# VectorE's order in 73 steps of a talking-heads attention kernel: the maximum ahead of the emptying

## The chip, the cores and the metric

The program runs on one core of a Trainium2 chip. The metric is device time in microseconds (us) from start to end of one execution.

## What is computed

Attention with mixing over the heads, and behind it two matrix products with a squared ReLU in between. Batch 4, 12 heads, 448 positions, head size 64; 1792 tokens of 768 channels, hidden size 2048.

```python
scores = scale * np.matmul(q, k.transpose(0, 1, 3, 2))
scores = np.einsum('bhij,hg->bgij', scores, w_pre)
scores = scores - np.max(scores, axis=-1, keepdims=True)
attn = np.exp(scores)
attn = attn / (np.sum(attn, axis=-1, keepdims=True) + 1e-09)
attn = np.einsum('bhij,hg->bgij', attn, w_post)
x = np.matmul(attn, v)          # then (batch, seq, heads * head size)
...
h = x @ w_in
r = np.maximum(h, 0.0)
out = (s * (r * r) + b) @ w_out
```

## The kernel before

The rows of the queries are cut into 16 chunks of 110 or 118 rows (four to a batch), and each chunk into 11 or 12 blocks of up to 10 rows; there are 180 blocks. A block holds 10 rows times 12 heads, 120 partitions, by 448 keys. The mixing over heads is then one matrix product of a block with a 120 x 120 matrix.

Values that need more than one matmul pass of precision are kept as two parts, a rounded high part and the rest, the low part. ScalarE copies a tile out of PSUM and makes the high part, and VectorE makes the low part by a subtraction (`low_parts`, L236 to L239). So a transposed q (`Tq`) or k (`Tk`) is ready for its matmuls only when VectorE has done its low part.

The attention runs as one loop over steps `s`. A block goes through several steps:

- step t: `premix(t)`: three matmuls into `pm` (L602), the maximum of each row on VectorE (L604, `st<-pm`), the exponential on ScalarE (L609, `pm<-pm,st`), which also sums, and the scaled sum (L613, `st<-pm`).
- step t+1: `normalize(t)`: the reciprocal on VectorE (L621) and the scaled high part on ScalarE (L623, `eh`); then `remainder(t)`, the low part of `eh`, on VectorE (L630).
- step t+3: `postmix(t)`: twelve matmuls into one of two buffers `po` (L645).
- step t+4: `evacuate(t)`: the emptying of `po` into `A` on VectorE (L661; on ScalarE for the last chunk).

Between these stand pieces of other work by a plan that is made ahead: `qk_pair`, the scores of the next but one chunk for two heads (six matmuls, L503 `sc<-Tk,Tq`, copied by ScalarE, L513 `S<-sc`); `av_pair` (L531, `xp<-A,v`) in front of it in the same step; and, mostly in the steps between, `prep_q` or `prep_k`, the transposes (L478 `trq`, L458 `trk`) into the same single PSUM buffer `sc` that the scores use, with their high part by ScalarE (L482, L462) and their low part by VectorE (L239), which is put on a list `later` and issued at the next `low_parts()`. The planned `qk_pair` steps come in most places every second step:

```python
w0, w1 = first[ci - 1] - LD, first[ci] - LD
return [w0 + i for i in (1, 3, 5, 7, 9, w1 - w0 - 1)]
```

Each engine works its instructions in the order in which the code issues them. VectorE also converts weights for the later products in between (`conversion`, L158 to L181, at most one piece in a step, ahead of the reciprocal; 49 pieces before the tail, spread over about 139 steps). The relayout of the scores into blocks (`blk<-S`) is a DMA on SP's queue, and GpSimd splits each block into its two parts (`hl`, L587 and L588).

Of the kernel before, what the change touches and what calls it, by code (L numbers as in the profile page):

```python
# [21 lines left out]
def talking_heads_attention__then__act_relu2_kernel(  # L22
# [53 lines left out]
    NB = len(blocks)  # L76
# [109 lines left out]
    def place_w(n):  # L186
        w_pool[n].tile([P, 2, 3 * P], F32R, tag=f"w{n}", name=f"place_{n}", bufs=1)

    def convert_step(upto):

        if done["run"] is None:
            if done["conv"] >= min(upto, len(units)):
                return False
            done["run"] = conversion(done["conv"])
        try:
            next(done["run"])
        except StopIteration:
            done["run"] = None
            done["conv"] += 1
        return True  # L200
# [13 lines left out]
    def load_x(r, b, kc):  # L214
        raw = rp.tile([P, S], F32, tag="xraw", name=f"xraw_{r}_{b}_{kc}", bufs=NKC)
        nc.sync.dma_start(raw, xd[b][kc])
        xraw_t[r, b, kc] = raw

    def split_x(r, b, kc):
        raw = xraw_t.pop((r, b, kc))  # L220
        if b == 1:

            if kc % 2 == 0:
                x_u["g"] = mp.tile(
                    [P, 2, PT], F32R, tag=f"g{kc // 2}_1", name=f"xg_{r}_{kc}", bufs=1
                )
            x = x_u["g"][:, :, kc % 2 * S:kc % 2 * S + S]
        else:
            x = rp.tile([P, 2, S], F32R, tag="x", name=f"x_{r}_{b}_{kc}", bufs=NKC)
        nc.scalar.activation(x[:, 0, :], raw, AF.Copy)  # L230
        later.append((x[:, 1, :], raw, x[:, 0, :]))
        x_u[r, b, kc] = x
# [3 lines left out]
    def low_parts():  # L236
        while later:
            o, x, hi = later.pop(0)
            nc.vector.tensor_tensor(out=o, in0=x, in1=hi.bitcast(F32), op=ALU.subtract)  # L239
# [322 lines left out]
    def qk_pair(ci, p):  # L562
        low_parts()
        for m in range(3):
            qk_part(ci, p, m)
# [9 lines left out]
    def relayout(t):  # L575
        ci, i0, ni = blocks[t]
        blk = blkp.tile([BP, S], F32, tag="blk", name=f"blk_{t}", bufs=LD)
        nb = first[ci + 1] - first[ci]
        r = t - first[ci]
        nc.sync.dma_start(blk[:ni * H, :], s_t[ci][r:r + nb * (ni - 1) + 1:nb, :, :])  # L580
        blk_t[t] = blk

    def split(t):
        n = blocks[t][2] * H
        blk = blk_t.pop(t)
        hl = blkp.tile([BP, 2, S], F32R, tag="hl", name=f"hl_{t}", bufs=2)
        nc.gpsimd.tensor_scalar(hl[:n, 0, :], blk[:n], 1.0, 0.0, op0=ALU.mult, op1=ALU.add)  # L587
        nc.gpsimd.tensor_tensor(  # L588
            out=hl[:n, 1, :], in0=blk[:n], in1=hl[:n, 0, :].bitcast(F32), op=ALU.subtract
        )  # L590
        hl_t[t] = hl

    def premix(t):
        n = blocks[t][2] * H
        hl = hl_t.pop(t)

        tag = "px" if t % 3 == 2 else "pm"
        pm = ps.tile([P, 512], F32, tag=tag, name=f"pm_{t}", bufs=banks.count(tag))
        for _ in range(2 if t < first[1] - 1 else 1 if t < first[1] + 3 else 0):
            nc.tensor.matmul(pm, keep[:, :P], keep, start=True, stop=True)  # L600
        for m, (w, x) in enumerate(((wpre_lo, 0), (wpre_hi, 1), (wpre_hi, 0))):
            nc.tensor.matmul(pm[:n, :S], w[:n, :n], hl[:n, x, :], start=(m == 0), stop=(m == 2))  # L602
        st = smp.tile([BP, 4], F32, tag="st", name=f"st_{t}")
        nc.vector.tensor_reduce(  # L604
            out=st[:n, 0:1], in_=pm[:n, :S], axis=AX.X, op=ALU.max, negate=True
        )

        e = pm[:, :S]
        nc.scalar.activation(e[:n], e[:n], AF.Exp, bias=st[:n, 0:1], accum_out=pm[:n, S:S + 1])  # L609
        e_t[t] = (e, st)  # L610

        total = pm[:, S:S + 1]
        nc.scalar.activation(  # L613
            st[:n, 2:3], total[:n], AF.Copy, scale=2.0 ** -15, bias=1e-9 * 2.0 ** -15
        )

    def normalize(t):

        n = blocks[t][2] * H
        e, st = e_t[t]  # L620
        nc.vector.reciprocal(st[:n, 3:4], st[:n, 2:3])  # L621
        eh = blkp.tile([BP, 2, S], F16, tag="eh", name=f"eh_{t}", bufs=3)
        nc.scalar.activation(eh[:n, 0, :], e[:n], AF.Copy, scale=st[:n, 3:4])  # L623
        eh_t[t] = eh

    def remainder(t):
        n = blocks[t][2] * H
        e, st = e_t.pop(t)
        eh = eh_t[t]
        nc.vector.scalar_tensor_tensor(  # L630
            out=eh[:n, 1, :], in0=e[:n], scalar=st[:n, 3:4], in1=eh[:n, 0, :],
            op0=ALU.mult, op1=ALU.subtract,
        )

    def postmix(t):
        ci, i0, ni = blocks[t]
        n = ni * H
        eh = eh_t.pop(t)
        if i0 == 0:
            a_t[ci] = ap_.tile([P, NC, H, CH], F32, tag="A", name=f"A_{ci}")  # L640
        po = ps.tile([P, 512], F32, tag="po", name=f"po_{t}", bufs=2)
        for c in range(NC):
            j0 = min(c * P, S - P)
            for m, (x, y) in enumerate(((1, 0), (0, 1), (0, 0))):
                nc.tensor.matmul(  # L645
                    po[:, c * BP:(c + 1) * BP],
                    eh[:n, x, j0:j0 + P],
                    wpost[:n, y].rearrange("p g i -> p (g i)"),
                    start=(m == 0),
                    stop=(m == 2),  # L650
                )
        po_t[t] = po

    def evacuate(t):
        ci, i0, ni = blocks[t]
        dst = a_t[ci][:, :, :, i0:i0 + ni]
        src = po_t.pop(t)[:, :NC * BP].rearrange("p (c g i) -> p c g i", c=NC, g=H)[:, :, :, :ni]
        if ci == NCH - 1:
            nc.scalar.activation(dst, src, AF.Copy)  # L659
        else:  # L660
            nc.vector.tensor_copy(dst, src)  # L661
# [6 lines left out]
    XA = 3  # L668
# [3 lines left out]
    plan, load = [], {}  # L672
# [95 lines left out]
    def run_plan(step, early):  # L768

        k0 = state["next"]  # L770
        while k0 < len(plan) and plan[k0][0] < step + 1:
            _, order, _, f, args = plan[k0]
            if (order == 0) == early:
                f(*args)
            k0 += 1
        if not early:
            state["next"] = k0
            copy_x()
# [55 lines left out]
    while plan[0][0] < 0:  # L834
        x = plan.pop(0)
        x[3](*x[4])
        low_parts()
    tail = first[NCH - 1]
    for s in range(NB + 4):
        if s == tail - LD:  # L840
            early.close()
            rp = ctx.enter_context(tc.tile_pool(name="rp", bufs=1, side="right", reuse_waits="tile"))
            rp.tile([P, S], F32, tag="xraw", name="place_xraw", bufs=NKC)
            for n in range(NU_EARLY, NU_EARLY + NU_TAIL):
                w_pool[n] = rp
                place_w(n)
            rp.tile([P, X_GAP // 4], F32, tag="gap", name="gap_x", bufs=1)
            rp.tile([P, 2, S], F32R, tag="x", name="place_x", bufs=NKC)
            rp.tile([P, END_GAP // 4], F32, tag="end", name="gap_end", bufs=1)
        if s + LD < NB:  # L850
            relayout(s + LD)
        if s + LS < NB:
            split(s + LS)
        if 0 <= s - 1 < NB:
            ops = 7 * NU_EARLY
            if not later and turn["ops"] < ops * (s - CONV0) / (tail - LD - 2 * NP - CONV0):
                turn["ops"] += convert_step(NU_EARLY)
            normalize(s - 1)
        if 0 <= s - 4 < NB:
            evacuate(s - 4)  # L860
        if s <= tail - XA:
            low_parts()
        if s < NB:
            premix(s)
        low_parts()
        if s < 2:
            (build_scale, build_post)[s](*loaded_consts)
            qk_pair(1, NP - 2 + s)
        if 0 <= s - 1 < NB:
            remainder(s - 1)  # L870
        run_plan(s, True)
        if 0 <= s - 3 < NB:
            postmix(s - 3)
        run_plan(s, False)
        if 0 <= s - (tail - LD) < NKC // 2:
            for kc in range(2):
                load_x(0, 0, 2 * (s - (tail - LD)) + kc)
        if 0 <= s - (tail - XA) < NKC:
            split_x(0, 0, s - (tail - XA))
        if 0 <= s - tail < NKC:  # L880
            load_x(0, 1, s - tail)
# [111 lines left out]
```

## Time and profile before

| | us |
|---|---|
| time, median of 3 runs (936.03 to 936.42) | 936.33 |
| time of the profiled execution | 936.44 |
| its span from first to last instruction | 934.7 |
| TensorE (PE) busy in it | 913.4 |
| VectorE (DVE) busy | 655.5 |
| ScalarE (ACT) busy | 567.1 |
| GpSimd (POOL) busy | 396.6 |

TensorE's granted clock is 1.00 in every part of the profile, the higher of its two levels. The attention loop fills about the first 470 us; then come the two matrix products, each in two halves. Busy time of TensorE is modelled at the ends of matmuls, so spacing from start to start says more than the printed gaps.

### The profile page before, as it was taken

To read this page: it belongs to the slowest core of one execution; us is meant where nothing else is said; L and a number is where in the kernel's file an instruction comes from. 1 tells how busy PE (TensorE), PEld (TensorE's weight loads), DVE (VectorE), ACT (ScalarE), POOL (GpSimd) and SP (SyncE) were. 2 spreads that over 40 slices of the span, in tenths; PEclk is the share of its full clock that TensorE was granted. 3 is DMA by queue.
4 is the path that set the end of the run, shared out by engine and by line. 5 is a ranking of instruction groups with operands and counts; after the bars stand their busy time and mean duration, and the time that the engine had idled before them with its cause. 6 is when DMAs were issued, how large, how long until landed. Compare 5 with 4: busy or idle time off the path is not lost.

```text
span 934.7 us, 19915 instructions
## 1 busy us (share of the span) xinstructions
PE 913.4 (98%) x7538; PEld 785.5 (84%) x7538; DVE 655.5 (70%) x1366; ACT 567.1 (61%) x1266; POOL 396.6 (42%) x452
## 2 busy tenths in 40 slices
PE   8899999999999999999999999999999999999998
PEld 5567777777777777777799999999999999999998
DVE  4888888889888898889688149966306924976211
ACT  5778788887888878888876877121117687700000
POOL 4776676666766666777523233000002333300000
PEclk9999999999999999999999999999999999999999
DMA  5755546564465635646324122353510420245321
GB/s 128 183 153 129 164 117 163 147 158 134 132 171 153 150 119 141 169 114 192 95 75 153 61 64 81 102 172 115 177 51 18 149 88 18 82 155 186 128 87 58
DMA packets 126556, 115.22 MB, mean 123 GB/s; under 512 B 63960, under 2 KB 122348, under 8 KB 126460
## 3 DMA queue, kind: packets, MB, share of 16 engines
q1 hardware_dynamic: 116934, 102.28, 39.5%
q10 hardware_dynamic: 9366, 11.59, 3.5%
q8 instruction: 59, 0.97, 0.5%
q0 software_dynamic: 160, 0.09, 0.1%
q14 instruction: 37, 0.30, 0.1%
HBM read 58.87 MB, written 16.52 MB: 81 GB/s over the span
## 4 chain that ended last, share of the span: by engine, by line
PE 62%; ACT 20%; DVE 11%; DMA 4%; issue 1%; POOL 0%; SPq 0%; ACTq 0%; DVEq 0%
PE po L311 25%; PE ph L254 24%; ACT pm L609 7%; ACT S L513 5%; ACT eh L623 4%; DVE A L661 4%; DMA blk<-S 4%; PE pm L602 4%; DVE st L604 3%; PE sc L503 3%; PE xp L531 3%; PE po L645 2%; ACT st L613 2%; ACT xs L553 1%; PE ph_head L254 1%; DVE Tq L239 1%
## 5 line engine op out<-in xcount | busy, mean ns | idle before, releaser
L311 PE MATMUL po<-w,g 128*128 128x384 f32 x1344 | 233.5, 336 | 0.0
L311 PEld LDWEIGHTS po<-w,g 128*128 128x128 f32 x1344 | 233.0, 188 | 0.3 <-ACT ob L318 0.3
L588 POOL TENSOR_TENSOR hl<-blk,hl 120x448 fp32r<-120x448 f32 x180 | 205.8, 1143 | 15.0
L272 POOL TENSOR_TENSOR g<-h,g 128x448 fp32r<-128x448 f32 x64 | 79.4, 1241 | 280.0 <-ACT g L271 260.2
L254 PE MATMUL ph<-x,w 128*128 128x448 f32 x810 | 164.1, 362 | 0.0
L254 PEld LDWEIGHTS ph<-x,w 128*128 128x128 f32 x810 | 151.9, 187 | 10.3
L587 POOL TENSOR_SCALAR hl<-blk 120x448 fp32r<-120x448 f32 x180 | 104.6, 581 | 120.5 <-PE pm L602 105.5
L645 PEld LDWEIGHTS <-eh 120*128 120x128 f16 (+1 forms) x2160 | 115.3, 98 | 40.8 <-issue 40.5
L645 PE MATMUL po<-wpost,eh 120*128 120x120 f16 (+1 forms) x2160 | 144.6, 217 | 1.4 <-ACT A L659 1.4
L609 ACT ACTIVATE pm<-pm,st 120x448 f32<-120x448 f32 x180 | 110.0, 611 | 56.6 <-DVE st L604 56.2
L630 DVE SCALAR_TENSOR_TENSOR eh<-pm,st,eh 120x448 f16<-120x448 f32 x180 | 122.3, 679 | 26.2 <-ACT eh L623 22.9
L623 ACT ACTIVATE eh<-pm,st 120x448 f16<-120x448 f32 x180 | 114.4, 636 | 15.4 <-DVE st L621 15.0
L604 DVE TENSOR_REDUCE st<-pm 120x1 f32<-120x448 f32 x180 | 110.6, 615 | 7.2 <-PE pm L602 6.9
L661 DVE COPY A<-po 128x480 f32<-128x480 f32 x168 | 107.0, 637 | 0.1
L602 PE MATMUL pm<-hl,wpre_hi 120*120 120x448 f32 x360 | 101.9, 364 | 0.7 <-POOL hl L588 0.7
L531 PE MATMUL xp<-A,v 128*64 128x110 f32 (+1 forms) x1536 | 93.5, 265 | 0.0
L503 PE MATMUL sc<-Tk,Tq 64*110 64x448 f32 (+1 forms) x576 | 82.7, 393 | 8.0 <-DVE Tq L239 5.0
L513 ACT ACTIVATE S<-sc 110x896 f32<-110x896 f32 (+1 forms) x91 | 83.1, 914 | 9.5 <-PE sc L503 6.5
L602 PE MATMUL pm<-hl,wpre_lo 120*120 120x448 f32 x180 | 82.8, 460 | 0.1
L531 PEld LDWEIGHTS xp<-A,v 128*64 128x64 f32 x1536 | 74.2, 136 | 9.6 <-issue 0.9
L318 ACT ACTIVATE ob<-po 128x384 f32<-128x384 f32 x28 | 13.8, 491 | 98.0 <-PE po L311 84.3
L602 PEld LDWEIGHTS pm<-hl,wpre_hi 120*120 120x120 f32 x360 | 65.4, 182 | 5.6 <-POOL hl L588 1.0
(81 smaller groups left out, 979.5 us busy)
## 6 DMA issues: line engine op xcount, KB each, us to landing
blk<-S SPq DMA_DIRECT2D x172, 210.0 KB
raw<-in_moe_w_in_dram SPq DMA_DIRECT2D x32, 384.0 KB
raw<-in_moe_w_out_dram SPq DMA_DIRECT2D x32, 384.0 KB
xraw<-xd SPq DMA_DIRECT2D x48, 224.0 KB
part<-ob ACTq DMA_DIRECT2D x28, 192.0 KB
acc<-part SPq DMA_DIRECT2D x28, 192.0 KB
out_dram<-acc ACTq DMA_DIRECT2D x28, 192.0 KB
v<-in_v_dram SPq DMA_DIRECT2D x24, 192.0 KB
```

The source lines that it names most:

```text
L254: nc.tensor.matmul(ph[:, :S], w[:, i, c0:c0 + P], x[:, y, :], start=(kc == 0 and m == 0), stop=(kc == NKC - 1 and m == 2),)
L311: nc.tensor.matmul(po[:, :NO], g[:, x, c0:c0 + P], w[:, y, :], start=(f == 0 and m == 0), stop=(f == NF - 1 and m == 2),)
L513: nc.scalar.activation(s_t[ci][:n, 2 * p:2 * p + 2, :], x_t["two"][:n, :, :S], AF.Copy, scale=SCALE)
L531: nc.tensor.matmul(xp[e * D:(e + 1) * D, p % 4, :n], vt[:, e, c, :], a[:, c, 2 * p + e, :n], start=(c == 0), stop=(c == NC - 1),)
L588: nc.gpsimd.tensor_tensor(out=hl[:n, 1, :], in0=blk[:n], in1=hl[:n, 0, :].bitcast(F32), op=ALU.subtract)
L602: nc.tensor.matmul(pm[:n, :S], w[:n, :n], hl[:n, x, :], start=(m == 0), stop=(m == 2))
L604: nc.vector.tensor_reduce(out=st[:n, 0:1], in_=pm[:n, :S], axis=AX.X, op=ALU.max, negate=True)
L609: nc.scalar.activation(e[:n], e[:n], AF.Exp, bias=st[:n, 0:1], accum_out=pm[:n, S:S + 1])
L623: nc.scalar.activation(eh[:n, 0, :], e[:n], AF.Copy, scale=st[:n, 3:4])
L630: nc.vector.scalar_tensor_tensor(out=eh[:n, 1, :], in0=e[:n], scalar=st[:n, 3:4], in1=eh[:n, 0, :], op0=ALU.mult, op1=ALU.subtract,)
L645: nc.tensor.matmul(po[:, c * BP:(c + 1) * BP], eh[:n, x, j0:j0 + P], wpost[:n, y].rearrange("p g i -> p (g i)"), start=(m == 0), stop=(m = ...
L661: nc.vector.tensor_copy(dst, src)
```

## The change

`pairs` are the steps in which the plan has a `qk_pair`; `full` are those of them that stand behind a step without one, up to the tail. In a full step VectorE gets its maximum (in `premix`) first, then the low parts, then the emptying of `po`. In all other steps the order stays emptying, low parts, maximum.

```diff
     tail = first[NCH - 1]
+    pairs = {x[0] for x in plan if x[3] is qk_pair}
+    full = {s for s in pairs if s - 1 not in pairs and s <= tail - XA}
     for s in range(NB + 4):
...
             normalize(s - 1)
-        if 0 <= s - 4 < NB:
-            evacuate(s - 4)
-        if s <= tail - XA:
-            low_parts()
+        if s not in full:
+            if 0 <= s - 4 < NB:
+                evacuate(s - 4)
+            if s <= tail - XA:
+                low_parts()
         if s < NB:
             premix(s)
         low_parts()
+        if s in full and 0 <= s - 4 < NB:
+            evacuate(s - 4)
```

There are 73 full steps; in 45 of them low parts stand between the maximum and the emptying. The instructions of PE, ACT, POOL and SP keep their order word for word, apart from the numbers in buffers' names; only VectorE's rows move. The numbers behind a name are its block (or chunk and part) and a running number of the buffer.

VectorE in step 43, a full step without low parts, from the reciprocal of block 42 to its remainder, before:

```order
L621 RECIPROCAL st_42_2183<-st_42_2183 120x1
L661 COPY A_3_1929<-po_39_2188 128x48x10
L604 TENSOR_REDUCE st_43_2214<-pm_43_2210 108x1
L630 SCALAR_TENSOR_TENSOR eh_42_2207<-pm_42_2179,st_42_2183,eh_42_2207 120x448
L175 SCALAR_TENSOR_TENSOR raw_1_649<-raw_1_649 128x384
L621 RECIPROCAL st_43_2214<-st_43_2214 108x1
```

and of the change:

```order
L621 RECIPROCAL st_42_2183<-st_42_2183 120x1
L604 TENSOR_REDUCE st_43_2213<-pm_43_2209 108x1
L661 COPY A_3_1929<-po_39_2188 128x48x10
L630 SCALAR_TENSOR_TENSOR eh_42_2207<-pm_42_2179,st_42_2183,eh_42_2207 120x448
L175 SCALAR_TENSOR_TENSOR raw_1_649<-raw_1_649 128x384
L621 RECIPROCAL st_43_2213<-st_43_2213 108x1
```

The emptying of block 39 and the maximum of block 43 have changed places; a conversion piece (L175) stands behind the remainder in both.

VectorE in step 45, a full step with a low part (of `Tq` of chunk 5), from the reciprocal of block 44 to that of block 45, before:

```order
L621 RECIPROCAL st_44_2264<-st_44_2264 108x1
L661 COPY A_3_1929<-po_41_2269 128x48x10
L239 TENSOR_TENSOR Tq_5_2032<-trq_5_1_2282,Tq_5_2032 128x2x110
L604 TENSOR_REDUCE st_45_2300<-pm_45_2296 120x1
L630 SCALAR_TENSOR_TENSOR eh_44_2292<-pm_44_2260,st_44_2264,eh_44_2292 108x448
L621 RECIPROCAL st_45_2300<-st_45_2300 120x1
```

and of the change:

```order
L621 RECIPROCAL st_44_2264<-st_44_2264 108x1
L604 TENSOR_REDUCE st_45_2298<-pm_45_2294 120x1
L239 TENSOR_TENSOR Tq_5_2032<-trq_5_1_2282,Tq_5_2032 128x2x110
L661 COPY A_3_1929<-po_41_2269 128x48x10
L630 SCALAR_TENSOR_TENSOR eh_44_2292<-pm_44_2260,st_44_2264,eh_44_2292 108x448
L621 RECIPROCAL st_45_2298<-st_45_2298 120x1
```

The maximum of block 45 has moved up two places, the emptying of block 41 down two; the low part keeps its place.

## Rows read from the trace of the kernel before

**Rows 1.** Windows view, two stretches: length, engines' busy us (instructions), PEclk, DMA share, GB/s.

```profile
26.00:66.00 40.00, 34.80 (x343) 25.31 (x340) 35.39 (x73) 30.57 (x79) 29.61 (x39) 1.00 0.65 167
66.00:440.00 374.00, 366.64 (x4194) 278.25 (x4192) 325.48 (x701) 305.34 (x770) 259.79 (x305) 1.00 0.55 147
```

**Rows 2.** Waits, whole span: who waited for whom, us in all, times, longest.

```profile
PEld sc L503 <- DVE Tq L239: 9.7, 20, 0.7
...
PE sc L503 <- DVE Tq L239: 5.0, 16, 0.6
PEld trq L478 <- ACT S L513: 4.7, 7, 1.6
PEld sc L503 <- DVE Tk L239: 4.5, 11, 0.9
...
PE trq L478 <- ACT S L513: 3.4, 5, 1.4
...
PE sc L503 <- DVE Tk L239: 1.2, 3, 0.7
```

**Rows 3.** Waits of ScalarE and VectorE, 66 to 440 us.

```profile
ACT pm L609 <- DVE st L604: 48.1, 73, 0.9
...
DVE eh L630 <- ACT eh L623: 20.1, 39, 1.0
DVE st L621 <- ACT st L613: 16.9, 61, 0.4
```

**Rows 4.** Timeline of TensorE, steps 43 to 47: start, duration, instruction, [idle before].

```profile
128.99 0.97 PE L531 MATMUL xp<-A,v 128*64 128x110 f32 x16
129.89 0.86 PE L503 MATMUL sc<-Tk,Tq 64*110 64x448 f32 x6
...
131.40 0.81 PE L645 MATMUL po<-wpost,eh 120*128 120x120 f16 x12
132.44 0.41 PE L478 MATMUL trq<-ident,nq 110*128 110x110 f32 x2 [0.23 <-ACT S L513]
...
134.04 0.97 PE L531 MATMUL xp<-A,v 128*64 128x110 f32 x16
135.29 0.86 PE L503 MATMUL sc<-Tk,Tq 64*110 64x448 f32 x6 [0.27 <-DVE Tq L239]
...
136.78 0.81 PE L645 MATMUL po<-wpost,eh 108*128 108x120 f16 x12
137.40 0.44 PE L602 MATMUL pm<-hl,wpre_lo 120*120 120x448 f32 x1
```

**Rows 5.** Timeline of VectorE, steps 43 to 45.

```profile
129.42 0.16 DVE L621 RECIPROCAL st<-st 120x1 f32<-120x1 f32 x1
...
130.06 0.61 DVE L604 TENSOR_REDUCE st<-pm 108x1 f32<-108x448 f32 x1
...
131.18 0.55 DVE L175 SCALAR_TENSOR_TENSOR raw<-raw 128x384 uint32<-128x384 uint32 x1
131.65 0.15 DVE L621 RECIPROCAL st<-st 108x1 f32<-108x1 f32 x1
...
132.27 0.61 DVE L604 TENSOR_REDUCE st<-pm 108x1 f32<-108x448 f32 x1
...
134.22 0.16 DVE L621 RECIPROCAL st<-st 108x1 f32<-108x1 f32 x1
134.30 0.64 DVE L661 COPY A<-po 128x480 f32<-128x480 f32 x1
134.85 0.38 DVE L239 TENSOR_TENSOR Tq<-trq,Tq 128x220 fp32r<-128x220 f32 x1
```

**Rows 6.** Timeline of ScalarE, steps 43 and 44.

```profile
130.71 0.61 ACT L609 ACTIVATE pm<-pm,st 108x448 f32<-108x448 f32 x1 [0.39 <-DVE st L604]
...
131.47 0.91 ACT L513 ACTIVATE S<-sc 110x896 f32<-110x896 f32 x1
...
133.29 0.63 ACT L609 ACTIVATE pm<-pm,st 108x448 f32<-108x448 f32 x1
```

## The prediction

> **What bounds the kernel now.** I read the windows view first, by stage [rows 1]. Between 66 and 440 us TensorE is busy for 366.64 of 374.00 us and VectorE for 325.48. In the opening stretch, 26 to 66 us, TensorE idles 5.2 us of 40. The two matrix products behind 470 us have no q k step and nothing that the change moves; they are left out below. Next comes the list of waits, for TensorE and its weight loads [rows 2]: where TensorE stands still in the attention stage, it stands in two places. Either q k waits for VectorE's low parts of Tq or Tk, or the transposes for Tq (`trq`) wait for ScalarE's copy of the scores, since the scores and the transposes share one buffer (`sc`). The matmul rows give 5.0 + 1.2 + 3.4 = 9.6 us, the weight-load rows of the same places 9.7 + 4.5 + 4.7 = 18.9 us. The first is too little, because matmul ends are modelled and overlap the gap. The second is too much, because a weight load also idles while the matmul before it still runs.
>
> Third, what ScalarE and VectorE wait for [rows 3]. Before its exponential (`pm`) ScalarE waits 48.1 us for VectorE's maximum (`st` L604), 73 times at 0.66 us each. VectorE in its turn waits 20.1 and 16.9 us for ScalarE. So these two pass a chain back and forth: maximum, exponential, sum, reciprocal, (emptying), maximum. TensorE is held by it only in the two places above.
>
> Last, the timelines of one pair of steps with what stands before and behind, blocks 43 to 46 [rows 4 to 6]. In step 43 the maximum (130.06) is ready to run at the reciprocal of 129.42, but the emptying (`A<-po`) is in front. The exponential follows at 130.71, and the copy of the scores, behind it in ScalarE's order, at 131.47, though the scores' matmuls began at 129.89. The transposes of step 44 could start 0.62 us after their post-mix began (as the next group does in the pair 136.78, 137.40), so at 132.02. They start at 132.44: a stall of 0.42 by spacing, of which the row prints 0.23. In step 45 q k could follow the a v group by 0.90 (128.99 to 129.89), so at 134.94. It starts at 135.29: 0.35 stalled, 0.27 printed. So spacing shows 0.77 where the rows print 0.50, and for the whole program I take 9.6 x 0.77 / 0.50 = 14.8 us of stall, between the two sums of rows 2.
>
> **The change, part by part.** It removes and adds no instruction. PE, ACT, POOL and the DMA queues keep their order. In 73 steps, those with a planned q k behind a step without one, VectorE's order becomes reciprocal, maximum, low parts, emptying, where it was reciprocal, emptying, low parts, maximum. In 45 of the 73 there are low parts in between.
>
> *The maximum, earlier.* The emptying starts 0.08 behind the reciprocal (134.22, 134.30) and the next instruction 0.55 behind that (134.85) [rows 5]. So the maximum of a full step without low parts comes 0.55 earlier, and with them by that and the low parts' own slot. For step 43: reciprocal 129.42, maximum 129.50 in place of 130.06, exponential 130.15, copy of the scores 130.91 in place of 131.47. TensorE then starts the transposes when it is ready, at 132.02: 0.42 won.
>
> *What of it reaches q k.* The exponential of step 44 stands 1.82 behind the copy of the scores on ScalarE (131.47 to 133.29) [rows 6] and would move to 132.73. But it also needs its maximum. A conversion piece (131.18) runs before the reciprocal of step 43 at 131.65, and that stays where it is; so the maximum of 44 stays at 132.27 and its exponential can come at 132.92 (0.65 behind, as 130.06 to 130.71). That is 0.37 earlier, and so is the reciprocal, 133.85. Now the full step 45: maximum 133.93, low part behind it at 134.48 (the copy's slot of 0.55 taken for the maximum's), q k 0.44 later (134.85 to 135.29), at 134.92. TensorE, 0.42 earlier, would want it at 134.52, so 0.40 of stall stays. The pair wins 0.37 of 0.77, 48%. Without the conversion the reciprocal of 43 follows its sum, the exponential of 44 goes to 132.73, and everything behind it moves 0.56: 73%. There are 49 conversion pieces before the tail, one at most in a step, over about 139 steps: 35% of steps. The mean is 0.35 x 48% + 0.65 x 73% = 64%, and 64% of 14.8 us is 9.5 us.
>
> *The low parts, in place of the emptying behind the maximum.* Their place in VectorE's row is the same, second behind the reciprocal, and 0.61 of maximum or 0.64 of copy in front is one price: nothing. But they now stand behind an instruction that waits for the pre-mix on TensorE, and q k waits behind them. In step 45 TensorE has the post-mix behind it too and is at the a v group by 134.04 - 0.42 = 133.62 [rows 4], so its pre-mix is long through at the maximum's turn, 133.93. Where the reciprocal came so early that the pre-mix held the maximum, q k would not yet be due. I take nothing for it.
>
> *The emptying, later.* In step 45 it moves from 134.30 to behind the low part: 134.48 + 0.38 at most, 134.86, done at 135.50. Its reader, the post-mix of step 46, stood at 136.78 and comes 0.37 earlier, 136.41. About 0.9 us of cover: nothing.
>
> *The remainder, reciprocal and conversions* keep their turn behind the same sum of instructions: nothing.
>
> The sum is 936.44 (the profiled execution) - 9.5 = 926.9; the median of the runs shown, 936.33, is 0.11 below it. I say 927.0.
>
> **Rivals.** *A, it is handed back.* What ScalarE wins at the transposes makes q k due earlier, and VectorE stays late in every pair as in the pair with the conversion. Taking 48% of the 9.6 us printed, 4.6 us is won: 931.8, and less if later pairs give some back. For it: VectorE is busy 87% of the stage [rows 1].
>
> *B, no change.* VectorE itself is the limit between 66 and 440 us, its instructions are the same, and a new order only moves its gaps: 936.3. For it: 325.48 of 374.00 us. Against it: of the 48.5 us that VectorE is idle, 37.0 go to waits for ScalarE [rows 3], which the new order shortens. The Trainium skill, page "Perfetto Trace Analysis", section "Identifying the Most-Contended Engine", would point there: it takes the engine with the highest occupancy as the one to shorten, and for TensorE it wants the share of weight loads, not matmul busy time. By that TensorE would stand at 278.25 of 374.00 us, 74%, below VectorE, and the time would stay 936.3; the trace speaks against it in so far as matmul groups that wait for nothing follow at a fixed spacing (0.62, 0.90 above), which leaves no such reserve.
>
> *C, slower.* The emptying comes too late for its reader. The post-mix two blocks on writes the same `po` buffer of two; if the emptying in the 45 steps with low parts ends more than 0.9 us later than worked out, TensorE stalls in the step behind each. Beyond that point 0.1 us costs 45 x 0.1 = 4.5 us, so 0.25 us takes 9.5 back with 1.8 on top: 938.2. For it: conversions and low parts can fall into one step. Against it: VectorE's sum in the step stays, and the reciprocal comes earlier.
>
> *D, more.* If the chain between ScalarE and VectorE gives way altogether, all stalls go: 14.8 to 18.9 us, 921.6 to 917.5.
>
> **How the numbers follow.** The forecast, 48% to all of the estimated stall with TensorE's spacing kept, has 0.64 and spans 936.4 - 14.8 = 921.6 to 936.4 - 7.1 = 929.3 (48% of 14.8). A has 0.10 (929.3 to 934.4), D 0.10, B 0.10, C 0.06. The range leaves out most of D, B, C and A's end: 921.0 to 933.0. A measurement of this kernel can tell about 0.2%, 1.9 us, from no change. Faster by more than that are the forecast, A and D, 0.84; same 0.10; slower 0.06.
>
> **What would show it.** Right: ScalarE's wait before the exponential falls from 48.1 us to below 20; the wait of `trq` for the copy of the scores all but goes; q k's waits for Tq and Tk fall by about half; the steps with an unhindered TensorE keep their spacing (0.90 from a v to q k); no row of the post-mix waiting for VectorE appears. Wrong: post-mix waits for `A<-po` (C); VectorE's idle time stays at 48 us while q k waits as long as now (B); the `trq` wait goes and q k's grows by as much (A).

## The result, and the profile after

| | us |
|---|---|
| before, median of 5 runs (936.03 to 939.25) | 936.42 |
| the change, median of 5 runs (927.10 to 927.79) | 927.54 |
| ratio, with 95% interval | 0.9898 (0.9883 to 0.9913) |
| profiled execution of the change, and its span | 927.10, 925.4 |

The change is 8.9 us faster, 1.0%; 927.0 was forecast. In a later group of runs the same kernel gave 927.37 us and a ratio of 0.9901 (0.9884 to 0.9918).

The chain that ended last, by engine, on the page of the kernel before and then on that of the change:

```profile
PE 62%; ACT 20%; DVE 11%; DMA 4%; issue 1%; POOL 0%; SPq 0%; ACTq 0%; DVEq 0%
```

```profile
PE 88%; ACT 4%; DVE 3%; DMA 2%; issue 1%; POOL 1%; ACTq 0%; POOLq 0%
```

Before, this chain ran through ScalarE and VectorE for 31% of the span, in the attention loop; now it runs through TensorE nearly all the way. The windows view of the change, in the two stretches of [rows 1] (it is ahead by then, so each holds a little more work):

```profile
26.00:66.00 40.00, 36.59 (x364) 26.52 (x363) 35.63 (x76) 31.06 (x80) 30.73 (x40) 1.00 0.68 174
66.00:440.00 374.00, 370.09 (x4281) 284.28 (x4281) 333.85 (x713) 310.96 (x786) 264.75 (x310) 1.00 0.56 150
```

TensorE's idle time falls from 5.2 to 3.4 us in the first and from 7.4 to 3.9 us in the second. The waits over the whole span, against [rows 2]:

```profile
ACT S L513 <- PE sc L503: 39.5, 71, 1.0
...
PEld sc L503 <- issue: 8.6, 34, 0.7
...
PE sc L503 <- DVE Tq L239: 2.5, 9, 0.7
...
PEld L645 <- DVE A L661: 1.7, 7, 0.4
...
PEld trq L478 <- ACT S L513: 1.2, 3, 0.5
...
PEld sc L503 <- DVE Tk L239: 1.0, 2, 0.5
```

The wait of the transposes for the copy of the scores was 4.7 us at the weight loads and is 1.2. The copy of the scores now waits for q k (39.5 us, in 71 of 91 copies; 6.5 us, in 13, before), where it used to wait behind a late exponential. For q k itself these rows do not tell what was won: the weight-load row for Tq, 9.7 us before, is 0.5 now, but the row that names nobody (`issue`) has grown from 2.0 to 8.6. The spacing below tells more. A few post-mixes wait for the emptying, 1.7 us in all, which is rival C's mechanism at a harmless size; the prediction had said that no such row would appear. And from 66 to 440 us, against [rows 3]:

```profile
DVE eh L630 <- ACT eh L623: 14.4, 33, 1.0
...
DVE st L621 <- ACT st L613: 10.9, 40, 0.5
...
DVE st L604 <- PE pm L602: 8.9, 16, 0.9
...
ACT pm L609 <- DVE st L604: 4.8, 15, 0.4
```

ScalarE's wait before the exponential has gone from 48.1 to 4.8 us.

The same pair of steps, 43 to 45, in timelines of TensorE, VectorE and ScalarE:

```profile
124.86 0.97 PE L531 MATMUL xp<-A,v 128*64 128x110 f32 x16
125.76 0.86 PE L503 MATMUL sc<-Tk,Tq 64*110 64x448 f32 x6
...
127.26 0.81 PE L645 MATMUL po<-wpost,eh 120*128 120x120 f16 x12
127.91 0.36 PE L478 MATMUL trq<-ident,nq 110*128 110x110 f32 x2
...
129.47 0.97 PE L531 MATMUL xp<-A,v 128*64 128x110 f32 x16
130.55 0.86 PE L503 MATMUL sc<-Tk,Tq 64*110 64x448 f32 x6
```

```profile
124.78 0.16 DVE L621 RECIPROCAL st<-st 120x1 f32<-120x1 f32 x1
124.86 0.60 DVE L604 TENSOR_REDUCE st<-pm 108x1 f32<-108x448 f32 x1
...
126.54 0.55 DVE L175 SCALAR_TENSOR_TENSOR raw<-raw 128x384 uint32<-128x384 uint32 x1
127.01 0.16 DVE L621 RECIPROCAL st<-st 108x1 f32<-108x1 f32 x1
...
127.63 0.62 DVE L604 TENSOR_REDUCE st<-pm 108x1 f32<-108x448 f32 x1
...
129.42 0.16 DVE L621 RECIPROCAL st<-st 108x1 f32<-108x1 f32 x1
129.50 0.60 DVE L604 TENSOR_REDUCE st<-pm 120x1 f32<-120x448 f32 x1
130.02 0.38 DVE L239 TENSOR_TENSOR Tq<-trq,Tq 128x220 fp32r<-128x220 f32 x1
130.32 0.65 DVE L661 COPY A<-po 128x480 f32<-128x480 f32 x1
```

```profile
126.67 0.92 ACT L513 ACTIVATE S<-sc 110x896 f32<-110x896 f32 x1 [0.23 <-PE sc L503]
127.48 0.62 ACT L553 ACTIVATE xs<-xp,xscale 128x440 f32<-128x440 f32 x1
127.99 0.64 ACT L623 ACTIVATE eh<-pm,st 108x448 f16<-108x448 f32 x1
128.51 0.62 ACT L609 ACTIVATE pm<-pm,st 108x448 f32<-108x448 f32 x1
```

Counted from the start of the a v group of step 43 (128.99 before, 124.86 here), in us:

| start of | before | as predicted | measured |
|---|---|---|---|
| copy of the scores, step 43 | 2.48 | 1.92 | 1.81 |
| transposes, step 44 | 3.45 | 3.03 | 3.05 |
| maximum of block 44 | 3.28 | 3.28 | 2.77 |
| exponential of block 44 | 4.30 | 3.93 | 3.65 |
| reciprocal of block 44 | 5.23 | 4.86 | 4.56 |
| q k of step 45 | 6.30 | 5.93 | 5.69 |

The transposes start 0.65 behind the start of the post-mix, without a wait. The q k still stands 0.18 us, since it starts 1.08 behind a v and not 0.90.

To compare whole kernels I take the spacing on TensorE's timeline, from the start of the pre-mix of block 7 to that of block 160, where nearly all planned q k steps lie. The stall of the transposes is what lies between the start of a post-mix and the first transpose beyond 0.62 us; that of q k is what lies between the starts of a v and q k beyond 0.90; both are summed over all steps of the stretch in the profiled execution.

| kernel | stretch, us | transposes stalled | q k stalled | rest |
|---|---|---|---|---|
| before | 380.3 | 7.9 | 9.4 | 363.0 |
| the change | 371.5 | 2.5 | 6.3 | 362.7 |
| e1, only steps without low parts | 373.8 | 3.5 | 6.7 | 363.6 |
| e2, only steps with low parts | 376.2 | 5.3 | 8.5 | 362.4 |
| e3, low parts, maximum, emptying | 372.3 | 3.8 | 5.2 | 363.3 |
| e4, low parts, emptying, maximum | 389.2 | 21.2 | 3.2 | 364.8 |
| e5, one copy more ahead | 403.0 | 3.9 | 34.1 | 365.0 |
| e6, one copy more behind | 393.2 | 0.9 | 26.0 | 366.3 |
| e7, all steps | 373.5 | 1.7 | 5.5 | 366.3 |
| e8, xs first | 368.1 | 2.7 | 2.8 | 362.6 |
| e9, xs first, VectorE as before | 382.1 | 17.1 | 2.1 | 362.9 |
| e10, conversions later | 372.0 | 3.1 | 6.6 | 362.3 |
| e11, both | 374.4 | 5.8 | 3.4 | 365.2 |
| e12, the change again | 371.1 | 2.6 | 6.2 | 362.3 |

The rest is 362.3 to 363.6 us in most rows, so there the two stalls carry the differences; in e4 to e7 and e11 it is 2.1 to 3.6 us longer than with the change. The stretch is 8.8 us shorter with the change: 5.4 from the transposes, 3.1 from q k. The rows are of one execution each; those of e2 and e11 were the slowest of five (933.25 and 930.63 us), that of e4 the fastest of four (944.90).

Some of both columns is spacing and not a wait. In no kernel do the transposes follow their post-mix sooner than 0.64, and 18 of the 78 q k groups, the same in every kernel, never follow a v sooner than 0.96. That makes 45 x 0.02 and 18 x 0.06, about 2.0 us in each row (0.9 and 1.1). Without it the waits are about 15.3 us before and 6.8 with the change.

### The profile page after: what moved, and what is told of

The parts are those of the page before. It is cut to its first block, busy times and chain, and to the rows that moved or that the text cites. A ratio compares the mean times of both kernels' runs of the same rounds, so it can differ in the third digit from the quotient of the medians.

```text
span 925.4 us, 19960 instructions
## 1 busy us (share of the span) xinstructions
PE 909.3 (98%) x7538; PEld 784.9 (85%) x7538; DVE 655.4 (71%) x1366; ACT 566.6 (61%) x1266; POOL 396.4 (43%) x452
## 4 chain that ended last, share of the span: by engine, by line
PE 88%; ACT 4%; DVE 3%; DMA 2%; issue 1%; POOL 1%; ACTq 0%; POOLq 0%
PE po L311 25%; PE ph L254 24%; PE pm L602 11%; PE po L645 10%; PE xp L531 8%; PE sc L503 7%; DMA blk<-S 2%; PE ph_head L254 1%; PE trk L458 1%; ACT pm L609 1%; ACT eh L623 1%; ACT S L513 1%; DVE st L604 1%; PE trq L478 1%; ACT xs L553 1%
## 5 line engine op out<-in xcount | busy, mean ns | idle before, releaser
L311 PE MATMUL po<-w,g 128*128 128x384 f32 x1344 | 233.5, 336 | 0.0
L311 PEld LDWEIGHTS po<-w,g 128*128 128x128 f32 x1344 | 233.0, 188 | 0.3 <-ACT ob L318 0.3
L588 POOL TENSOR_TENSOR hl<-blk,hl 120x448 fp32r<-120x448 f32 x180 | 206.5, 1147 | 15.0
L254 PE MATMUL ph<-x,w 128*128 128x448 f32 x810 | 164.0, 362 | 0.0
L254 PEld LDWEIGHTS ph<-x,w 128*128 128x128 f32 x810 | 151.9, 188 | 10.2
L513 ACT ACTIVATE S<-sc 110x896 f32<-110x896 f32 (+1 forms) x91 | 83.6, 919 | 44.4 <-PE sc L503 39.5
```

Of the source, the lines that this page charges most:

```text
L254: nc.tensor.matmul(ph[:, :S], w[:, i, c0:c0 + P], x[:, y, :], start=(kc == 0 and m == 0), stop=(kc == NKC - 1 and m == 2),)
L311: nc.tensor.matmul(po[:, :NO], g[:, x, c0:c0 + P], w[:, y, :], start=(f == 0 and m == 0), stop=(f == NF - 1 and m == 2),)
L588: nc.gpsimd.tensor_tensor(out=hl[:n, 1, :], in0=blk[:n], in1=hl[:n, 0, :].bitcast(F32), op=ALU.subtract)
```

## The experiments

Theory 1 is that of the prediction: the maximum ahead of the emptying brings the exponential, and behind it on ScalarE the copy of the scores, forward; the transposes win first, q k one step later. Theory 2: what counts is q k's own wait for the low parts in the full step. Theory 3 is rival B: VectorE's occupancy is the limit. All ratios below are against the kernel before.

**e1 and e2, one kind of full step alone.** `later` holds the low parts that wait.

```diff
+        now = s in full and not later      # e1; e2: and bool(later)
-        if s not in full:
+        if not now:
...
-        if s in full and 0 <= s - 4 < NB:
+        if now and 0 <= s - 4 < NB:
```

e1: 

> The new order only in the 28 full steps that have no low parts waiting; the other 45 keep the order of before. Theory 1 (the exponential, and behind it on ScalarE the copy of the scores, come earlier; the transposes of the next step gain first, q k one step later): each of these steps moves its maximum by one slot of 0.55 us, and the long waits of the transposes (1.4 and 1.2 us at the opening, 0.4 to 0.6 us later) stand behind such steps. About half of the 8.9 us, so 931 to 933 us. Theory 2 (what counts is the wait of q k for the low parts in the full step itself, with the maximum out of the way): nothing here has low parts, so 936. The sum of what this kernel and the next one win should be near the whole of 8.9 us if the two kinds of step act apart, and above it if one kind's gain hides the other's.

e2: 

> The new order only in the 45 full steps that have low parts waiting. Theory 1: the maximum moves by 0.55 us and by the low parts' slot, so the copy of the scores of these steps is held by q k alone; the transposes' waits behind steps without low parts stay (about half of 5.5 us), q k's waits fall from 9.5 to about 6.5 us. 929 to 931 us. Theory 2: all of the gain is here, 927.5 us.

Measured: e1 930.45 us, 0.9947 (0.9935 to 0.9959); e2 932.03 us, 0.9953 (0.9940 to 0.9966). By medians the 28 steps without low parts win 5.7 us and the 45 with them 4.1, by the ratios 5.0 and 4.4, with intervals that overlap. So each kind wins about half, and together they win 9.4 to 9.7 us where both at once win 8.9 (9.5 by the ratio): they act nearly apart. Theory 2 would have all of it in e2, and nothing in e1; yet e1, where no low part changes place, wins and takes q k's stall from 9.4 to 6.7 us. By its median e1 came out slightly better than I had it, and e2 worse.

**e3 and e4, the low parts first.** Full steps only; the lines give VectorE's order in words.

```diff
-        maximum, low parts, emptying
+        low parts, maximum, emptying     # e3
+        low parts, emptying, maximum     # e4
```

e3: 

> In the full steps VectorE takes low parts, maximum, emptying (the change: maximum, low parts, emptying). The maximum is still ahead of the emptying, but behind the low parts, which wait for ScalarE's copy of the transposes some 0.3 us longer than the reciprocal does. Theory 1: the maximum comes 0.5 to 0.9 us later than in the change, so the copy of the scores is held by the exponential in some steps again: 1 to 2 us slower than the change, 928.5 to 929.5 us. Theory 2: the low parts one slot of 0.53 us earlier take away most of the 6.2 us for which q k still waits: 922 to 924 us.

e4: 

> In the full steps VectorE takes low parts, emptying, maximum: against before only the low parts and the emptying have changed places, the maximum stays last. Theory 1: q k may win a little, but the maximum is later than before by the time for which the low parts wait for ScalarE (0.1 to 0.4 us), and with it the exponential, the copy of the scores and the transposes: 2 to 8 us slower than before, 938 to 944 us. Theory 2: the low parts 0.4 us earlier win 3 to 4 us of q k's waits: 932 to 933 us.

Measured: e3 929.52 us, 0.9930 (0.9916 to 0.9944); e4 946.29 us, 1.0106 (1.0093 to 1.0119). ScalarE's wait for the maximum over the whole span in the kernel before, and then the waits of e4:

```profile
ACT pm L609 <- DVE st L604: 56.2, 84, 2.5
```

```profile
ACT pm L609 <- DVE st L604: 69.2, 83, 2.2
...
PE trq L478 <- ACT S L513: 9.3, 17, 1.4
...
PE trk L458 <- ACT S L513: 5.0, 13, 0.7
...
PEld sc L503 <- DVE Tq L239: 3.4, 12, 0.5
...
PEld sc L503 <- DVE Tk L239: 2.2, 5, 0.7
```

This is the sharpest test. In e4 q k's stall falls to a third (9.4 to 3.2 us), as theory 2 wants, and the kernel is 10 us slower, since ScalarE waits longer for the maximum (69.2 us, 56.2 before) and the transposes stall 21.2 us. TensorE, held there, also comes to q k later, so the smaller stall at q k is no gain by itself. Theory 2 falls. The loss is larger than the 2 to 8 us that I gave theory 1. e3 is where theory 1 put it: the maximum ahead of the emptying keeps most of the gain, the low parts ahead of it cost about 2 us.

**e5 and e6, one more copy in each full step.** It writes the same values into `A` once more; the result does not change.

```diff
+        if s in full and 0 <= s - 4 < NB:
+            dummy(s - 4)                   # e5: here, ahead of premix(s)
...
         low_parts()
         if s in full and 0 <= s - 4 < NB:
+            dummy(s - 4)                   # e6: here instead
             evacuate(s - 4)
```

e5: 

> The change, with one more copy of the same po into the same place of A in each of the 73 full steps, ahead of the maximum: 73 x 0.55 = 40 us more work for VectorE, and the maximum where it stood before. Theory 1: the place decides. The maximum of the full steps is as late as before, and VectorE's other work 0.55 us later: the gain is lost, and some more, 935 to 940 us. Theory 3 (VectorE's occupancy is the limit, and the order only moves its gaps): the same as in the next kernel, whatever the place.

e6: 

> The same 73 more copies, but behind the maximum and the low parts, just ahead of the emptying. Theory 1: the chain from maximum to copy of the scores is untouched in its own step, and the emptying still has some 0.4 us to its reader; what is lost comes from the reciprocal of the next step being 0.55 us later where VectorE has no gap: 1 to 4 us slower than the change, 928.5 to 931.5 us, and at least 4 us faster than the kernel before this one. Theory 3: both kernels with more work are slower alike, by a good part of 40 us.

Measured: e5 958.94 us, 1.0238 (1.0224 to 1.0252); e6 949.61 us, 1.0142 (1.0128 to 1.0156). Both numbers of theory 1 are missed. The place is worth 9.3 us, as much as the change itself, so theory 3 in its pure form (the same whatever the place) falls. But the work behind the chain, 40 us as I counted it and 34.8 us of busy time (690.2 against 655.4), cost 22 us where I had 1 to 4. The page of e6, the chain by engine, its windows view, 66 to 440 us, and its waits, whole span (`A` L667 is the emptying in this kernel):

```profile
PE 58%; DVE 31%; ACT 9%; issue 1%; DMA 0%; POOL 0%; ACTq 0%; DVEq 0%
```

```profile
66.00:440.00 374.00, 352.02 (x4051) 269.19 (x4048) 347.83 (x743) 301.02 (x743) 254.43 (x293) 1.00 0.52 139
```

```profile
PE sc L503 <- DVE Tq L239: 14.9, 27, 1.3
...
PE sc L503 <- DVE Tk L239: 8.3, 15, 0.7
...
PEld L645 <- DVE A L667: 6.3, 16, 1.1
```

VectorE is busy 93%. The two products behind the loop take 48% of the chain (L311 and L254), and VectorE 31 of the other 52; q k waits for its low parts. Half of theory 3 stays: at 87 to 89% VectorE has little room, and added work there is paid for by more than half (22 of 34.8 us in e6, 31 of 37.8 in e5). A part of e6's loss is the emptying itself, which comes one copy later: the post-mix waits 6.3 us for it, 1.7 with the change.

**e7, the new order in all steps up to the tail.**

```diff
-        if s not in full:
+        if s > tail - XA:
...
-        if s in full and 0 <= s - 4 < NB:
+        if s <= tail - XA and 0 <= s - 4 < NB:
```

> The maximum ahead of low parts and emptying in all steps up to the tail, not in the 73 alone. In a short step the reciprocal is ready about as early as the pre-mix is through, so the maximum often waits there for TensorE with the emptying behind it. Theory 1: the short steps' maximum is not what the copy of the scores waits for; a gain of up to 0.55 us on the exponential of the short step can reach q k, against emptyings and remainders that come later: within 2 us of the change, 926.5 to 929.5 us. If the alternation were the point (a full step needs the opposite of a short one), it is several us slower than the change.

Measured: 929.96 us, 0.9934 (0.9920 to 0.9948), 2.4 us slower than the change and a little outside what I gave. Its waits, whole span (13.0 and 1.7 us with the change):

```profile
DVE st L604 <- PE pm L602: 52.5, 85, 1.9
...
PEld L645 <- DVE A L661: 11.2, 31, 0.5
```

In the short steps the maximum comes to its turn before the pre-mix is through and holds the emptying behind it, and the post-mix then waits for that: rival C's mechanism, paid in the rest (366.3 us, 3.6 more), not in the two stalls (7.2, 1.6 less). So keeping the old order in the short steps is worth about 2 us; it is not the main point.

**e8 and e9, xs ahead of the copy of the scores on ScalarE**, with the change and with VectorE's order of before.

```diff
+            if f is qk_pair and not early:
+                copy_x()
             if (order == 0) == early:
                 f(*args)
```

e8: 

> The change, and on ScalarE the copy of the attention output (xs, 0.63 us, slot 0.51) issued ahead of the copy of the scores in the same step, where it stood behind it. With the change ScalarE idles 35.2 us in all (64 times, 0.55 each) before the copy of the scores, waiting for q k; the a v group that xs reads is done by then. Theory 1: the copy fits into that gap, and the chain copy of the scores, xs, high part, exponential, sum, reciprocal, maximum, low part, q k gets 0.51 us shorter in the 24 steps with xs, where q k's longest waits stand: 2 to 4.5 us faster than the change, 923 to 925.5 us. If q k's remaining waits come from elsewhere, 927.5 us; if xs delays the copy of the scores instead, slower.

e9: 

> The kernel before, with xs issued ahead of the copy of the scores on ScalarE as in the kernel that won 2.3 us on top of the change; VectorE's order is that of before. Theory 1: in the kernel before ScalarE has no gap in front of the copy of the scores (the exponential ends after q k), so xs delays that copy by 0.51 us in 24 steps; the transposes behind wait longer, q k's chain is as long as it was: no gain, 935.5 to 939 us. If xs first wins by itself, whatever the maximum does, 933.5 to 934.5 us.

Measured: e8 925.22 us, 0.9881 (0.9867 to 0.9894); e9 938.10 us, 1.0019 (1.0010 to 1.0028). Waits of e9, then of e8, whole span:

```profile
ACT S L513 <- PE sc L503: 8.9, 15, 1.0
PE trq L478 <- ACT S L513: 8.6, 17, 1.4
...
PEld sc L503 <- DVE Tq L239: 2.0, 4, 0.7
```

```profile
ACT S L513 <- PE sc L503: 33.7, 59, 1.0
...
PE sc L503 <- DVE Tq L239: 1.5, 3, 0.7
...
PE trq L478 <- ACT S L513: 0.9, 2, 0.6
```

In both q k's stall nearly goes (2.1 and 2.8 us, of which 1.1 is spacing). With VectorE's old order the transposes pay for it, 17.1 us; with the new one they don't, because ScalarE has the gap in front of the copy that the earlier exponential left. e8 is the fastest kernel of the study: 0.2% ahead of the change, all its four runs (924.50 to 925.89) below all ten of the change (926.47 to 929.00), though the two intervals of the ratio overlap and the two were not timed in one group.

**e10 and e11, the conversion pieces behind the maximum**, ahead of the remainder; e11 with xs first too.

```diff
-            if not later and turn["ops"] < ops * (...):
-                turn["ops"] += convert_step(NU_EARLY)
+            due = not later and turn["ops"] < ops * (...)
             normalize(s - 1)
...
         if 0 <= s - 1 < NB:
+            if due:
+                turn["ops"] += convert_step(NU_EARLY)
             remainder(s - 1)
```

e10: 

> The change, with the pieces of the weight conversion on VectorE moved from ahead of the reciprocal to just ahead of the remainder of the same step. In the timeline of the pair 43 to 45 the piece stands in front of the reciprocal of the short step and the remainder then waits 0.41 us for ScalarE, so the piece would fit into that wait. If conversions are what holds the remaining q k waits, as the prediction had it (48% of a pair won with one, 73% without), some 0.2 to 0.4 us is won in about a third of 45 pairs: 3 to 5 us, 923 to 925 us. If the chain over ScalarE (copy of the scores, xs, high part, exponential) holds them: 0 to 1.5 us, 926 to 927.5 us.

e11: 

> Both on top of the change: xs ahead of the copy of the scores, conversion pieces ahead of the remainder. If the two waits are one behind the other, the sum of both: 924 to 925 us or less; where xs alone has left less than 3 us of q k's waits, the conversions can give at most that: 922 to 925.2 us.

Measured: e10 928.01 us, 0.9913 (0.9899 to 0.9927); e11 928.41 us, 0.9915 (0.9901 to 0.9929). Moving the conversions wins nothing. By itself this does not clear them, since the new place might cost as much as the old one; that they are not what holds the remaining waits of q k is seen with the timelines of the single steps, below. e11 is 3 us slower than e8, which neither line of its expectation allowed; its transposes stall 5.8 us and its rest is 2.6 us longer. Of the 5.8 us, about 3 stand in three steps (64, 75 and 109). In two of these its trace shows the copy of the scores waiting 1.8 and 2.5 us for the DMA of the relayout; in the change that DMA costs the copy 0.9 us in one of them. Why the relayout is late there, and what makes the rest longer, is open.

**e12, the change again.** 

> The change itself once more, since the kernels above were timed in other groups than it was: 0.988 to 0.991 of the time before (925.5 to 928 us), so that the kernel with xs first (0.9881) stays ahead of it or within its interval. Theory 1 and its rivals say the same here.

Measured: 927.37 us, 0.9901 (0.9884 to 0.9918), as expected.

## Why the prediction was right

*The place of the gain.* Right. The long waits were at the transposes and at q k, and these two make up 8.5 of the 8.8 us of the stretch. e4 shows that the transposes' part hangs on the maximum, through the copy of the scores, and not on the low parts.

*The sum.* 9.5 us were worked out and 8.9 measured. The stall was put at 14.8 us. By spacing over all steps of the stretch it is 17.3, of which about 2.0 is no wait: the 0.62 was read from a post-mix with a pre-mix behind it (136.78 to 137.40), and transposes take 0.64. With 15.3 us left, this term was nearly right, though it rested on a single pair. Of it 64% was to go, and 56% went (8.5 of 15.3): 5.4 of 7.0 us at the transposes, 3.1 of 8.3 at q k, where I had said about half. So the share is the term that was too large, and that it came as near as this is in part luck, as the next point shows.

*The split by conversion* is the step that failed. The pair that I worked out has a conversion piece in it and was to win 0.37 us at q k; it won 0.61. I had held the reciprocal of block 42 in place, but the pairs before had already brought it forward, from 0.43 behind the start of a v to 0.08 ahead of it, and the conversion with it. The timelines of all steps agree. Of the 44 full steps with low parts in the stretch, 25 have a conversion piece in front of the reciprocal in the short step before: 57%, where I had taken the 35% of all steps. Their stall at q k fell from 0.21 to 0.14 us each, that of the other 19 from 0.18 to 0.10. Both kinds won 0.07 to 0.08 us, where the working had 0.05 lost with a conversion (0.35 to 0.40) and 0.14 won without. And e10, which takes the conversions out of that place, wins nothing. What holds q k is the rest of the chain on ScalarE: copy of the scores, xs, high part, exponential, sum. With xs taken out of it (e8) the stall falls from 6.3 to 2.8 us.

*The emptying at no price.* Nearly right: seven post-mixes, each in the step behind a full one, wait for it, 1.7 us in all, and e7 shows what it costs where the cover is gone.

*Rival A* did not come: the stall of q k fell, too. *Rival B* was given 0.10 and has more in it than I allowed. The Trainium skill, page "Perfetto Trace Analysis", section "Identifying the Most-Contended Engine", takes the engine of highest occupancy as the one to shorten. VectorE's work did not change by the change (655.5 us busy before, 655.4 after), so by this rule alone nothing was to be won, and 8.9 us were. But e6 agrees with its other half: 34.8 us more of VectorE's busy time cost 22 us. *C* has a price in e7, and in e6 with more work in front of the emptying. *D* would need all stalls gone; e8 still has 5.5 us in the two columns, about 2.0 of them spacing.

## What to carry to other kernels

An engine that is nearly full can still hold others up by its order: find the instruction that another engine waits for most often (here ScalarE for the maximum, 73 times at 0.66 us), and ask what stands in front of it that nobody needs yet. Ask then what runs through the engine behind it: the gap that opens there may take other work, as it took xs, which would have cost time in the order before. Put an instruction that waits for another engine at the front only where it is ready in time; in the short steps it held up what stood behind it.

## What was not expected of the hardware

Conversion pieces on VectorE took longer in the change than before. The 49 pieces of the attention loop have a mean of 537 ns before, 607 in the change and 587 in e12, the same kernel again. One line alone misleads: the seven pieces of L175 have a mean of 601 ns before and 762 in the change, but 632 in e12. One of the seven took 1.44 us in the change, most of it beside GpSimd's second instruction on a block (L588); the rows of VectorE and GpSimd:

```profile
174.70 1.44 DVE L175 SCALAR_TENSOR_TENSOR raw<-raw 128x384 uint32<-128x384 uint32 x1
```

```profile
174.58 1.15 POOL L588 TENSOR_TENSOR hl<-blk,hl 120x448 fp32r<-120x448 f32 x1
```

This holds for all of them. In the kernel before, 33 of the 49 pieces do not overlap that instruction, and none of them takes more than 0.55 us; the other 16 have a mean of 661 ns and reach 1.08 us. In the change 26 do not overlap it, again with 0.55 us at most, and 23 do, with a mean of 759 ns. So the long pieces stand beside L588, and the new order puts more pieces there. That GpSimd is what holds them is not shown: no run moves the one without the other.
